# Respacing the attention bursts among the MoE matmuls, pairing a group's first two d_ff chunks in one PSUM tile, and computing the second scores unmixed

## Chip, cores, metric

One core of one Trainium2 chip. The metric is device time in microseconds; lower is better. Compared are fast runs of the same rounds on the same chip. "Stop" below means a pause of TensorE for which the profile names no releaser. A "pair" is a weight load with its matmul. A "page" is a block of 256 instructions, thus some 128 pairs of TensorE's program; a "packet" is the DMA transfer that brings one; a "boundary" is the place in the program where one page ends and the next begins, timed here by the last weight load of the page that ends.

## The reference, cut to what matters

```python
# attention: batch 8, heads 8, seq 576, head_dim 64
# q_d, k_d, v_d: means of 4 neighbouring rows (144 rows)
out = repeat(softmax(q_d k_d^T / 8) v_d, 4) + softmax(mask(|i - j| < 4, q k^T / 8)) v
x   = out as 4608 x 512
h   = x @ w_in                  # 512 x 2048
return (h * sigmoid(1.702 * h)) @ w_out   # 2048 x 512
```

## The kernel before

Nine groups of 512 tokens go through the MoE part, 64 matmuls of 512 columns for each of the two products. The attention of batch g+1 runs inside group g, in bursts of small matmuls put at given places (`POS`, counted in first-product chunks up to 16 and in second-product matmuls from there): scores of four heads and their exponentials (13, 16), scores of the other four heads (35), two bursts of attention times V, "AV" (42, 53), two of transposes (62, 71). Their result xT feeds the next group.

```python
PA = [psum.tile([128, 2, 512], FP32, name=f"pa{i}") for i in range(3)]   # attention, in rotation
PM = [psum.tile([128, 512], FP32, name=f"pm{i}") for i in range(2)]      # MoE, alternating

def scores_mixed(b, qd):
    sp = [ps_tile(), ps_tile()]          # 80 local score matmuls, two tiles
    sd = ps_tile()                       # 24 downsampled ones, a third tile
    ahead = {2 * kc: (lambda kc=kc: scores_d(b, qd, sd, [kc])) for kc in range(3)}
    return scores(b, qd, sp=sp, ahead=ahead), sd      # downsampled first, then in turn
# ... cut ...
def s_pe(qd):
    st["s", qd], st["d", qd] = scores_mixed(b, qd)

def s_act(qd):                           # ScalarE, VectorE
    exp_local(qd, st["s", qd])           # frees the two score tiles
    exp_down(qd, st["d", qd])            # frees the third
    mask_local(qd)
# ... cut ...
def mm1(g, gT, steps, first=0):
    for ffc in range(first, n_ffc):
        for f in steps.get(ffc, ()):
            f()
        hps = pm_tile() if g else acc[ffc] if ffc < 6 else late[ffc - 6]
        for dmc in range(n_dmc):
            hps_mm(g, ffc, dmc, hps)
        silu(gT, ffc, hps)
# ... cut ...
POS = [13, 16, 35, 42, 53, 62, 71]
POS_0 = [16, 18, 30, 48, 52, 57, 66, 70, 75]      # group 0
```

The softmax here doesn't subtract the row's maximum and nothing guards it: scores larger than these inputs give would overflow.

## Time and profile before

| | before |
|---|---|
| median of 3 runs | 323.8 us (323.51 to 324.85) |
| span of the profiled run, clock | 322.0 us, 1.00 |
| TensorE busy | 95% |
| groups 1 to 6, lengths | 34.5, 33.1, 34.3, 34.2, 33.1, 33.7 us |

The group lengths run from a group's first weight load to the next one's. All six hold the same work. The lines of the profile stand in the prediction. Two further sources are the trace's records themselves: the start and length of each 16,384-byte instruction packet, and the start of each weight load, counted from the program's beginning (4860 of them).

### The profile page before, as it was taken

To read this page: it belongs to the slowest core of one execution; us is meant where nothing else is said; L and a number is where in the kernel's file an instruction comes from. 1 tells how busy PE (TensorE), PEld (TensorE's weight loads), DVE (VectorE), ACT (ScalarE), POOL (GpSimd) and SP (SyncE) were. 2 spreads that over 40 slices of the span, in tenths; PEclk is the share of its full clock that TensorE was granted. 3 is DMA by queue.
4 is the path that set the end of the run, shared out by engine and by line. 5 is a ranking of instruction groups with operands and counts; after the bars stand their busy time and mean duration, and the time that the engine had idled before them with its cause. 6 is when DMAs were issued, how large, how long until landed. Compare 5 with 4: busy or idle time off the path is not lost.

```text
span 322.0 us, 10814 instructions
## 1 busy us (share of the span) xinstructions
PE 304.4 (95%) x4806; PEld 156.8 (49%) x4860; DVE 135.5 (42%) x224; ACT 184.0 (57%) x317; POOL 140.0 (43%) x172
## 2 busy tenths in 40 slices
PE   7999989999899999998999989999999999999995
PEld 3664544445444554454545544555445544444444
DVE  6973625912574077505770468027811650000000
ACT  4565762677456674667365836674677456415611
POOL 8993960299009920893059603980296000000000
PEclk9999999999999999999999999999999999999999
DMA  7999999899519941994169714981350210020012
GB/s 117 119 197 209 179 128 212 191 227 238 146 38 200 217 110 66 200 213 116 63 154 212 168 37 129 230 183 55 111 105 0 72 67 0 0 98 34 0 64 69
DMA packets 63550, 40.02 MB, mean 124 GB/s; under 512 B 44048, under 2 KB 54416, under 8 KB 63504
## 3 DMA queue, kind: packets, MB, share of 16 engines
q0 software_dynamic: 18864, 14.95, 32.0%
q1 hardware_dynamic: 44496, 24.32, 31.1%
q8 instruction: 38, 0.62, 0.8%
q14 instruction: 8, 0.07, 0.1%
q10 hardware_dynamic: 144, 0.07, 0.1%
HBM read 44.83 MB, written 9.44 MB: 169 GB/s over the span
## 4 chain that ended last, share of the span: by engine, by line
PE 89%; issue 4%; DMA 4%; DVE 1%; POOL 1%; ACT 0%; POOLq 0%; DVEq 0%
PE pm L702 36%; PE pm L758 34%; PE pa L375 3%; PE pa L702 2%; PE pa L758 2%; DMA qb<-in_q_dram 2%; PE pa L394 2%; PE pa L461 2%; PE pa L502 2%; PE pa L446 2%; DMA vb<-in_v_dram 1%; PE pm L773 1%; PE pa L487 1%; DVE y L478 1%; PE pa L590 1%
## 5 line engine op out<-in xcount | busy, mean ns | idle before, releaser
L702 PE MATMUL pm<-xT,w_in_bf 128*128 128x512 bf16 x527 | 119.7, 379 | 0.7
L758 PE MATMUL pm<-w_out_bf,gT 128*128 128x512 bf16 x493 | 114.3, 379 | 5.3 <-issue 5.1
L713 ACT ACTIVATE gT<-pm 128x512 bf16<-128x512 f32 x136 | 81.1, 598 | 44.0 <-PE pm L702 44.0
L702 PEld LDWEIGHTS <-w_in_bf 128*128 128x128 bf16 x576 | 55.6, 98 | 66.4 <-issue 0.4
L758 PEld LDWEIGHTS <-gT 128*128 128x128 bf16 x560 | 51.6, 98 | 59.6 <-issue 1.4
L425 DVE TENSOR_TENSOR es<-es,mask 128x600 bf16<-128x600 bf16 x28 | 20.2, 733 | 90.6 <-ACT es L411 89.8
L294 POOL TENSOR_TENSOR pq<-kT 128x576 f32<-128x576 bf16 x14 | 16.1, 1148 | 88.5 <-DVE kT L276 88.5
L743 ACT ACTIVATE osb<-pm 128x512 f32<-128x512 f32 (+2 forms) x35 | 20.8, 593 | 36.4 <-PE pm L758 32.4
L617 ACT COPY od<-pa 128x384 f32<-128x384 f32 (+1 forms) x56 | 18.5, 411 | 31.3 <-PE pa L487 25.5
L478 DVE TENSOR_TENSOR y<-pa,rc 128x896 bf16<-128x896 f32 x28 | 30.6, 1092 | 1.0
L638 DVE TENSOR_TENSOR xT<-pa,od 128x570 bf16<-128x570 f32 x28 | 21.1, 753 | 10.3 <-ACT od L617 10.2
L411 ACT ACTIVATE es<-pa 128x600 bf16<-128x600 f32 x32 | 19.7, 667 | 8.8 <-PE pa L375 8.7
L745 DVE TENSOR_SCALAR osb<-pm 128x128 f32<-128x128 f32 x1 | 0.3, 292 | 55.3 <-ACT osb L743 55.3
L314 POOL TENSOR_TENSOR v<-v 112x512 f32<-112x512 f32 x18 | 23.1, 1281 | 0.0
L276 DVE STREAM_TRANSPOSE kT<-kb 128x576 f32<-128x576 f32 x16 | 20.0, 1248 | 3.6 <-DMA kb<-in_k_dram 3.6
L276 DVE STREAM_TRANSPOSE qT<-qb 128x576 f32<-128x576 f32 x16 | 19.9, 1242 | 0.4
L375 PE MATMUL pa<-qT,kT 32*64 32x60 bf16 x1280 | 17.6, 199 | 1.4 <-DVE qT L276 1.4
L375 PEld LDWEIGHTS <-kT 32*64 32x64 bf16 x1280 | 15.9, 103 | 2.0 <-issue 1.5
L230 POOL DMA_DIRECT2D vb<-in_v_dram x20 | 13.7, 697 | 6.5 <-DMA w_in_bf<-in_moe_w_in_dram 4.3
L417 ACT ACTIVATE ed<-pa 128x864 bf16<-128x864 f32 x16 | 14.3, 896 | 2.0 <-PE pa L394 1.8
L394 PE MATMUL pa<-qdT,kdT 32*64 32x144 bf16 x384 | 15.1, 231 | 0.0
L294 POOL TENSOR_TENSOR pq<-qT 128x576 f32<-128x576 bf16 x13 | 15.1, 1159 | 0.0
(98 smaller groups left out, 267.2 us busy)
## 6 DMA issues: line engine op xcount, KB each, us to landing
out_dram<-osb SPq DMA_DIRECT2D x35, 256.0 KB, 2.1
vf<-in_v_dram SPq DMA_DIRECT2D x60, 128.0 KB, 5.2
v<-in_v_dram SPq DMA_DIRECT2D x36, 192.0 KB, 5.1
kb<-in_k_dram POOLq DMA_DIRECT2D x16, 288.0 KB, 7.7
qb<-in_q_dram POOLq DMA_DIRECT2D x16, 288.0 KB, 10.2
w_out_bf<-in_moe_w_out_dram POOLq DMA_DIRECT2D x4, 512.0 KB, 17.6
vb<-in_v_dram POOLq DMA_DIRECT2D x20, 64.0 KB, 5.4
w_in_bf<-in_moe_w_in_dram POOLq DMA_DIRECT2D x2, 512.0 KB, 6.3
```

Of the source, the lines that this page charges most:

```text
L276: nc.vector.transpose(out=t32.rearrange("p (i c) -> p c i", c=18), in_=store[b, qd].bitcast(FP32).rearrange("p (c d) -> p c d", c=18),)
L294: eng.tensor_tensor(out=t1, in0=sv[:, :, 0:2, :], in1=sv[:, :, 2:4, :], op=ALU.add)
L314: eng.tensor_tensor(out=t1[0:112], in0=x[:, :, 0:2, :], in1=x[:, :, 2:4, :], op=ALU.add)
L375: nc.tensor.matmul(sp[r // 2][64 * par : 64 * par + 64, r % 2, 60 * i : 60 * i + 60], lhsT=kT[b, qd][rows, k0 : k0 + 64, a], rhs=qT[b, qd] ...
L394: nc.tensor.matmul(bank[r // 2][64 * j : 64 * j + 64, SD * kc : SD * kc + SD], lhsT=kdT[qd][rows, 48 * kc : 48 * kc + 64, a], rhs=qdT[b, q ...
L425: nc.vector.tensor_tensor(out=ev, in0=ev, in1=mask, op=ALU.mult)
L478: nc.vector.tensor_tensor(out=y[:, xs], in0=ov[:, :, :, 0:D], in1=rc[:, xs].to_broadcast([128, n, 7, D]), op=ALU.mult,)
L638: eng.tensor_tensor(out=sub(xT[hp], t0 + 3, (57, 2), (114, 5), (1, 57)), in0=sub(x, 3, (509, 2), (57, 5), (1, 57)), in1=sub(od, 3, (57, 2) ...
L702: nc.tensor.matmul(acc, lhsT=w_in_bf[:, dmc, ffc * 128 : (ffc + 1) * 128], rhs=xT[dmc][:, g * TG : g * TG + TG], start=(dmc == 0), stop=(d ...
L713: nc.scalar.activation(out=gT[:, ffc, :], in_=acc, func=AF.Silu, scale=GELU_SCALE)
L743: eng.activation(out=osb, in_=ap, func=AF.Copy, scale=1.0 / GELU_SCALE)
L758: nc.tensor.matmul(ops[t], lhsT=gT[:, ffc, t * 128 : (t + 1) * 128], rhs=w_out_bf[:, ffc, :], start=(ffc == 0), stop=(ffc == n_ffc - 1),)
```

## The change

The intent: never so many small matmuls close together, and chunks and scores arranged so that the new places don't wait for ScalarE or xT.

```diff
-            st["s", qd], st["d", qd] = scores_mixed(b, qd)
+            if qd == 0:
+                st["s", qd], st["d", qd] = scores_mixed(b, qd)
+            else:
+                st["s", qd] = scores(b, qd)
+                st["d", qd] = scores_d(b, qd)
@@ mm1
+        if g > 1:
+            t = ps_tile()
+            for dmcs in (range(n_dmc - 1), (n_dmc - 1,)):
+                for ffc in range(2):
+                    for dmc in dmcs:
+                        hps_mm(g, ffc, dmc, t[:, ffc, :])
+            for ffc in range(2):
+                silu(gT, ffc, t[:, ffc, :])
+            first = 2
@@
-    POS = [13, 16, 35, 42, 53, 62, 71]
-    POS_0 = [16, 18, 30, 48, 52, 57, 66, 70, 75]
+    POS = [13, 16, 33, 44, 55, 65, 74]
+    POS_0 = [16, 18, 27, 48, 52, 57, 66, 70, 75]
```

## The prediction

> **What bounds the kernel now.** I read the page first, then the time per group, then the chain of work that ended last, then the single bursts on TensorE. The page:
>
> ```profile
> PE 304.4 (95%) x4806; PEld 156.8 (49%) x4860; DVE 135.5 (42%) x224; ACT 184.0 (57%) x317; POOL 140.0 (43%) x172
> ...
> q8 instruction: 38, 0.62, 0.8%
> ...
> PE 89%; issue 4%; DMA 4%; DVE 1%; POOL 1%; ACT 0%; POOLq 0%; DVEq 0%
> ...
> L702 PE MATMUL pm<-xT,w_in_bf 128*128 128x512 bf16 x527 | 119.7, 379 | 0.7
> L758 PE MATMUL pm<-w_out_bf,gT 128*128 128x512 bf16 x493 | 114.3, 379 | 5.3 <-issue 5.1
> ```
>
> TensorE is the bound: 89% of the chain is its own work. Matmuls overlap, so the 379 ns of one is not its cost: in the chain eight 128x512 matmuls take 1.72 to 1.73 us, so one costs 0.2155 us. 1152 such matmuls (nine groups of 128) make 248 us of 322.0; they, the attention's small matmuls and the head (some 24 us) leave few stalls. Only stalls and the cost of the bursts can change: no matmul is removed. The busy time of each engine in four groups shows how small the pool is:
>
> ```profile
> 95.09:128.21 33.12, 32.22 (x586) 16.56 (x592) 16.46 (x25) 20.95 (x36) 17.54 (x19) 1.00 0.71 144
> 128.21:162.47 34.26, 32.50 (x587) 16.69 (x592) 16.49 (x25) 20.95 (x36) 17.54 (x19) 1.00 0.64 141
> 162.47:196.64 34.17, 32.32 (x586) 16.62 (x592) 16.57 (x25) 20.95 (x36) 17.54 (x19) 1.00 0.65 140
> 196.64:229.73 33.09, 32.19 (x587) 16.55 (x592) 16.42 (x25) 20.95 (x36) 17.54 (x19) 1.00 0.64 145
> ```
>
> The work is the same, the lengths are not: 33.1 against 34.2 us (second column), all at clock 1.00. From the last MoE matmul before a burst to the first after it, less one matmul (each burst also misses one matmul record), a burst costs 1.17 us for the first scores, 1.25 for the second, 0.85 for each pair of attention times V (AV), 0.63 for each pair of transposes: 5.4 us, and 128 x 0.2155 + 5.4 = 33.0, which is the short group. The long ones hold this, in the chain of a window:
>
> ```profile
> 81.33 1.46 PE pm L758 x6
> 82.79 0.22 PE pa L461 x12
> 83.01 0.16 PE pa L446 x20
> 83.16 0.06 PE pa L461 x8
> 83.23 0.95 issue
> 84.18 0.22 PE pa L461 x4
> ```
>
> TensorE stops inside the AV burst, for nothing that another engine releases. Four groups have it (0.95 at 83.2, 0.85 at 150.3, 0.95 at 184.9, 0.27 at 251.9). Counted in weight loads, the stops come after number 1374, 2525, 3164 and 4315: differences of 1151, 640 and 1151, that is 9, 5 and 9 times 128, less 0 to 1. 128 pairs of load and matmul are 256 instructions, and the trace's 38 instruction packets are of 16,384 bytes each. So I read them as **waits for the next page of instructions**. The packet records agree: one ends at 82.79, 149.67, 184.36 and 250.71, and TensorE goes on at 84.18, 151.12, 185.84 and 252.17, 1.39 to 1.48 us later each time. Before these four stops a packet starts 0.9 to 1.7 us after the previous page boundary is executed (at 148.75 4.0 us after it, behind the V loads in small packets) and takes 0.92 to 1.3. A page that is used up in under some 3.5 to 4.2 us therefore stalls. The second scores (104 pairs), 7 MoE matmuls and the first AV (76 pairs) are 187 pairs in about 3.6 us: the one place that dense. In net burst time the stops cost 1.14, 1.05, 1.15 and 0.48 us, with 0.19 and 0.18 in the AV burst after two of them: 4.2 us in all.
>
> One more stall stands in group 0:
>
> ```profile
> 43.59 0.04 ACT es L411
> 43.63 0.53 issue
> 44.16 0.67 ACT es L411
> 44.84 0.04 issue
> 44.88 2.75 PE pa L758 x12
> ```
>
> There token tile 2 accumulates in a PSUM tile that the second scores used; after two MoE matmuls TensorE waits until ScalarE's exponential has read it, from 43.80 (43.58 plus one matmul) to 44.88: 1.08 us.
>
> **The Trainium skill.** "Runtime: NRT & Kernel Launch", Instruction fetch mechanics, says that instructions are refilled in 16 KiB blocks of 256, each engine's sequencer fetching the next through its own DMA queue; packets and spacing here agree. It also says that the fetch is hidden by the sequencer's pace; this trace differs, with 4.2 us of stops. "TensorE: Matmul & The Clock Gate", Wait — 56ns, not 53.3ns?, gives 215.7 ns between warm 512-column matmuls; the chain's 0.2155 agrees. "TensorEngine Tiling (Array Packing)", Key Properties, says that a change of tiling mode drains the array; each burst here loses about 0.09 us before and 0.13 after it. The number of bursts doesn't change, so neither does that. "DMA: Bandwidth & Descriptors", Queues, rings and completion order, has each DMA engine take turns between queues by packet; the late fetch at 148.75, when the V loads thin out, fits only partly.
>
> **The change, part by part.**
> 1. *Spacing.* In groups 1 to 6 the second scores come 2 matmuls earlier, the AVs 2 later, the transposes 3 later. Between second scores and first AV stand 11 MoE matmuls instead of 7: 4 x 0.2155 = 0.86 us more for the fetch. I counted the boundaries through the new instruction order: they stay at the same instruction numbers, so two pairs away within the bursts. The page at 1374 then lasts 3.7 instead of 2.9 us, against 4.2 needed: 0.3 to 0.5 is left of 1.14. That at 3164: 3.7 against 3.9, 0.2 to 0.3 left of 1.15. That at 4316: 3.7 against 3.3, nothing left of 0.48. That at 2525 begins in plain MoE work before the scores, so it gains only 2 matmuls, 0.43 us, and the V loads in front of its fetch may start later: 0.7 left of 1.05. The two small ones stay, 0.37. Left about 1.7 of 4.2: **-2.5 us**. No other page in the new order lasts under 3.7 us.
> 2. *Group 0.* Second scores 3 matmuls earlier (0.65 us), so five stand before tile 2. Unmixed, the 80 local score matmuls end about 0.25 us sooner within the burst, and so the exponential can start. 1.08 - 0.65 - 0.25, less the longer burst, leaves about nothing: **-1.0 us**. Unmixing is also what allows the earlier place: the tile of the downsampled scores is free only at 42.1 us, when its exponential ends (41.20 + 0.90), and the burst would now start at 41.6.
> 3. *Second scores not mixed.* In the head both kinds stand alone: 80 score matmuls take 0.77 us to the next work, 24 downsampled ones 0.51; with 0.09 of entry 1.37 us against 1.17 to 1.25 mixed. Seven times 0.12 to 0.2, less the 0.08 longer entry of the mixed second burst that may go: **+0.5 us**.
> 4. *Two d_ff chunks in a PSUM tile, fourth k step last.* Eight matmuls are reordered, none added. It moves the first use of xT[3] from the 4th to the 7th matmul of a group. Now the last transposes start 2.5 us before the group does, and the merges of xT[2] and xT[3] end 2.2 and 3.1 us after they start. In the new order 6 instead of 9 matmuls follow them: start to group 0.63 + 6 x 0.2155 = 1.9, with xT[2] used at 2.4 (merged 2.2) and xT[3] at 3.2 (3.1). It just fits: **0**. The PSUM tile is the second transpose's of the previous pair, read out more than a microsecond before.
>
> Sum: -2.5 - 1.0 + 0.5 = -3.0; 323.8 - 3.0 = 320.8 us.
>
> **The rivals.** *All fetch stops go:* the spacing may let the sequencer run ahead in the 11 matmuls and ask early; fetches in MoE stretches do start up to 1.3 us before their boundary is executed. Then -4.2 - 1.0 + 0.5: 319.1. *The stops move:* what was gained shows up at other boundaries, or behind the V loads, as the one at 150.3 was; fetch waits differ by over a microsecond from group to group. Then only group 0 and a little remain: 322.3. *A new wait at the start of a group:* the slack of 0.1 to 0.2 us in part 4 fails, because VectorE takes four merges in a row behind ScalarE's copies; 0.2 us in six groups, with later transposes of K and Q delaying GpSimd's pooling (now done 1.3 us before the first scores need it, then 0.7). That would add about 1.5: 322.3.
>
> **Range and chances.** The removable stalls are 4.2 + 1.1 = 5.3 us, or 1.6%, so over 2% faster would need something that the profile doesn't show. The range goes from all stops gone to nearly none. Predicted 320.8 us, 8 in 10 between 318.9 and 322.5; faster by over 2% 0.02, within 2% 0.97, slower 0.01.
>
> **What would show it.** Right: groups 1 to 6 near 33.2 to 33.6 us each; "issue" waits in the first AV gone or under 0.4 us, at weight loads still 128 apart; no wait on ScalarE's exponential in group 0; second scores 0.1 us dearer; no idle time before the first line of a group. Wrong: stops of the same size elsewhere, a wait of the MoE matmuls for xT, or a wait of the scores for GpSimd or ScalarE.

## The result, and the profile after

| | before | after |
|---|---|---|
| median of 5 runs each | 324.1 us | 320.82 us (320.37 to 322.2) |
| ratio of fast runs | | 0.9904 (0.9875 to 0.9932) |
| profiled span | 322.0 us | 319.4 us |
| groups 1 to 6 | 34.5, 33.1, 34.3, 34.2, 33.1, 33.7 | 34.0, 33.2, 33.4, 33.2, 33.2, 33.2 |

The busy time of each engine in groups 1 to 4 of the kernel after (stretch, length, then busy time of TensorE, weight loads, VectorE, ScalarE, GpSimd; clock, DMA share, GB/s):

```profile
60.20:94.23 34.03, 32.58 (x587) 16.67 (x592) 15.54 (x23) 21.41 (x37) 17.73 (x19) 1.00 0.74 176
94.23:127.43 33.20, 32.30 (x586) 16.57 (x592) 16.34 (x25) 20.83 (x36) 17.74 (x19) 1.00 0.69 144
127.43:160.79 33.36, 32.46 (x586) 16.68 (x592) 16.36 (x25) 20.83 (x36) 17.74 (x19) 1.00 0.67 144
160.79:194.00 33.21, 32.31 (x586) 16.57 (x592) 16.43 (x25) 20.83 (x36) 17.75 (x19) 1.00 0.66 144
```

Groups 3 and 4 have come down to the length of the short ones, group 1 only in part. The chain of work in group 1 shows what is left there:

```profile
83.13 0.16 PE pa L446 x20
83.29 0.06 PE pa L461 x6
83.35 0.54 issue
83.89 0.25 PE pa L461 x6
```

It is the same stop after the same weight load, number 1374, now 0.74 us longer than an undisturbed step instead of 1.14. In group 0 a stop of 0.55 us is new in this run, inside the third burst of transposes after weight load 990, 384 = 3 x 128 before 1374. (The kernel before was at the edge there: its packet landed 1.52 us before it was needed, where the stops go on 1.39 to 1.48 us after one. The run b_late below, whose group 0 is that of before, has a stop of 0.3 us at this place.) The wait of group 0 on ScalarE is gone; the same place in the chain (compare the lines of group 0 in the prediction):

```profile
43.06 0.16 issue
43.22 1.03 PE pm L771 x4
44.24 1.94 PE pa L771 x9
```

Token tile 2 (the first `pa L771`) follows without a pause. And something was added: ScalarE at the start of group 2.

```profile
94.43 0.60 ACT L756 ACTIVATE osb<-pm 128x512 f32<-128x512 f32 x1 [0.22 <-PE pm L771]
96.16 1.09 ACT L717 ACTIVATE gT<-pa 128x512 bf16<-128x512 f32 x2 [1.13 <-PE pa L706]
97.12 0.60 ACT L717 ACTIVATE gT<-pm 128x512 bf16<-128x512 f32 x1
```

ScalarE idles for 1.13 us and then gets both paired chunks at once, so it reads the third chunk (97.12) late. The run a_third below shows that this is what costs time: at the 17th matmul of groups 2 to 7 the distance between two MoE matmuls is 0.316 us instead of 0.216; group 8 loses about as much.

Added up from the bursts: stops 4.2 to 1.4 us (0.55 in group 0, 0.74 in group 1, 0.14 in group 3), -2.8; the wait of group 0, -1.08; the second scores, +0.08 in six groups and +0.16 in group 0, +0.64; the pair, seven times 0.1, +0.7. The sum is -2.5 us, where the spans differ by 2.6. The count of stops is rough by 0.2 us: pauses of 0.16 and 0.09 us in the second scores of groups 1 and 2 before are left out, the 0.14 us in those of group 3 after are in.

### The profile page after: what moved, and what is told of

The parts are those of the page before. It is cut to its first block, busy times and chain, and to the rows that moved or that the text cites. A ratio compares the mean times of both kernels' runs of the same rounds, so it can differ in the third digit from the quotient of the medians.

```text
span 319.4 us, 10815 instructions
## 1 busy us (share of the span) xinstructions
PE 305.1 (96%) x4806; PEld 156.9 (49%) x4860; DVE 135.0 (42%) x224; ACT 183.0 (57%) x317; POOL 140.9 (44%) x172
## 4 chain that ended last, share of the span: by engine, by line
PE 90%; DMA 4%; issue 3%; DVE 1%; POOL 1%; ACT 0%; POOLq 0%; DVEq 0%
PE pm L771 35%; PE pm L706 33%; PE pa L706 6%; PE pa L375 3%; PE pa L771 2%; DMA qb<-in_q_dram 2%; PE pa L394 2%; PE pa L461 2%; PE pa L502 2%; DMA vb<-in_v_dram 2%; PE pa L446 1%; PE pm L786 1%; PE pa L487 1%; DVE y L478 1%; PE pa L590 1%
## 5 line engine op out<-in xcount | busy, mean ns | idle before, releaser
L771 PE MATMUL pm<-w_out_bf,gT 128*128 128x512 bf16 x492 | 114.2, 379 | 5.3 <-issue 5.1
L706 PE MATMUL pm<-xT,w_in_bf 128*128 128x512 bf16 x472 | 108.6, 379 | 0.7
L717 ACT ACTIVATE gT<-pm 128x512 bf16<-128x512 f32 x122 | 72.7, 599 | 38.3 <-PE pm L706 38.2
L771 PEld LDWEIGHTS <-gT 128*128 128x128 bf16 x560 | 51.6, 98 | 59.0 <-issue 0.2
L314 POOL TENSOR_TENSOR v<-v 112x512 f32<-112x512 f32 x18 | 24.0, 1331 | 0.0
L706 PE MATMUL pa<-xT,w_in_bf 128*128 128x512 bf16 x88 | 21.1, 379 | 0.1
L717 ACT ACTIVATE gT<-pa 128x512 bf16<-128x512 f32 x22 | 12.2, 604 | 8.5 <-PE pa L706 8.4
L375 PE MATMUL pa<-qT,kT 32*64 32x60 bf16 x1280 | 15.5, 201 | 1.0 <-DVE qT L276 1.0
L375 PEld LDWEIGHTS <-kT 32*64 32x64 bf16 x1280 | 13.8, 103 | 4.6 <-DVE es L425 3.0
```

Source lines behind the costliest of these rows:

```text
L314: eng.tensor_tensor(out=t1[0:112], in0=x[:, :, 0:2, :], in1=x[:, :, 2:4, :], op=ALU.add)
L375: nc.tensor.matmul(sp[r // 2][64 * par : 64 * par + 64, r % 2, 60 * i : 60 * i + 60], lhsT=kT[b, qd][rows, k0 : k0 + 64, a], rhs=qT[b, qd] ...
L706: nc.tensor.matmul(acc, lhsT=w_in_bf[:, dmc, ffc * 128 : (ffc + 1) * 128], rhs=xT[dmc][:, g * TG : g * TG + TG], start=(dmc == 0), stop=(d ...
L717: nc.scalar.activation(out=gT[:, ffc, :], in_=acc, func=AF.Silu, scale=GELU_SCALE)
L771: nc.tensor.matmul(ops[t], lhsT=gT[:, ffc, t * 128 : (t + 1) * 128], rhs=w_out_bf[:, ffc, :], start=(ffc == 0), stop=(ffc == n_ffc - 1),)
```

## The experiments

Two accounts were to be told apart: **F**, that TensorE stops because the next page of instructions isn't there when a page has been used up, and **W**, that the stops belong to the AV burst and what it waits for. When the first results were in, a second question arose: which part of the change ended the stops. All kernels are correct unless it is said. Differences given against the kernel after are those of the two ratios to before, unless the same rounds held both. The profiled runs of a_oldpos, a_nopair and a_mixed have a mean clock of 0.989: the clock record shows half speed for 6.8 us in the head and at the start of group 0. From them only group lengths and waits after that are used. Of the timed runs, two of six of a_oldpos, one of four of a_nopair and two of four of a_mixed have this clock and are 1 to 4 us longer than the others, which stretches the ratios; the differences without them are given too. Where the stops of two kernels are compared, each count is of one profiled run.

**Moving the page boundaries (b_shift48).** The kernel before, with 48 more pairs of weight load and matmul in the head:

```diff
-    warm(4)
+    warm(2)
+    for n in range(52):
+        nc.tensor.matmul(PM[1][:, 0:64], lhsT=zero16[:, 0:128], rhs=zero16[:, 0:64],
+                         start=True, stop=True)
```

> The kernel before with 48 more pairs of weight load and matmul in its head (52 tiny ones in place of two warming matmuls), so that every later page boundary lies 48 pairs earlier in the work. Nothing else changes. Theory F (page fetch): the page that spans second scores and first AV is now short in groups 2 and 5 (boundaries at loads 1966 and 3756 of the old count) and long in groups 1, 3, 4 and 6: groups 2 and 5 grow from 33.1 to about 34.2 us, groups 1, 4 and 6 shrink to about 33.1; group 3 may keep a smaller stop at its transposes. Theory W (a wait for PSUM or another engine in the AV burst): the long groups stay 1, 3, 4 and 6.

Ratio 0.9971 (0.9915 to 1.0027). Groups 1 to 6 last 33.3, 34.5, 33.2, 34.7, 33.9, 33.0 us: groups 1, 3 and 6 have lost their stops, 2 and 5 have got one, after weight loads 2013, 3164 and 3804 (the 48 counted): remainders 93, 92 and 92 modulo 128, the same as before (91 to 94), so the same places in the count and other places in the work. (The remainder sinks because separate waits stand among the pairs in TensorE's queue; with those that the trace records counted as one instruction each, all these stops fall on one place modulo 256, to within one instruction.) The chain in group 2:

```profile
116.51 0.06 PE pa L461 x8
116.57 1.23 issue
117.80 0.22 PE pa L461 x4
```

Put plainly: the stop follows the count of instructions and not the work. That settles F against W. Group 4 was expected to be free and isn't (1.5 us at 183.9): its page lasted long enough, but its packet started only 3.98 us after the boundary before, with about 2,890 of V's 256-byte packets started meanwhile. The length of a page alone doesn't tell where a stop falls.

**The same shift in the changed kernel (a_shift48).**

> The changed kernel with the same 48 pairs in its head. Theory F: the stop of 0.73 us in group 1 and that of 0.54 us in group 0's transposes go, since their boundaries move; the most that groups 2 and 5 can show is 0.5 us each. Group 1 falls from 34.0 to 33.3. In all 0 to 1.3 us faster than the changed kernel, if the head isn't longer. Theory W: the stops stay in groups 0 and 1.

Ratio 0.9898 (0.9837 to 0.9959). Group 1 falls to 33.3 us and no group from 1 to 6 has a stop over 0.3 us; the stop in group 0's transposes goes too. But a new one of 1.0 us comes up inside group 0's second scores (0.86 us of "issue" at 42.69, after weight load 735, 640 = 5 x 128 before 1375). A pause of 0.25 us ahead of those scores is another thing, a wait for the DMA of w_out. The gain in one place is given back in the other. As expected where the stops went; that group 0 would take them up was not seen ahead.

**Old places in groups 1 to 6 (a_oldpos).**

```diff
-    POS = [13, 16, 33, 44, 55, 65, 74]
+    POS = [13, 16, 35, 42, 53, 62, 71]
```

> The changed kernel with the old places of the bursts in groups 1 to 6 (35, 42, 53, 62, 71); group 0, the unmixed second scores and the paired first chunks stay. Theory F (page fetch): the page of the second scores and the first AV lasts 2.8 us again, so the stops come back in groups 1, 3, 4 and 6 at weight loads 128 apart, about 3 us in all less what already remains (0.7): 2.5 to 3.5 us slower than the changed kernel, near 323.5 us. Theory W (what the change gained is group 0 and an earlier exponential through unmixing, the spacing is incidental): within 1 us of the changed kernel.

Ratio 0.9925 (0.9896 to 0.9954), 0.2% or some 0.7 us from the changed kernel (0.4 without the two runs at the lower clock), with intervals that overlap: no difference clear of noise. The 2.5 to 3.5 us of F were wrong, and the time lies within what was written for W. In the profile two of four stops came back, in group 1 (0.6 us) and in group 4:

```profile
187.53 0.09 PE pa L446 x10
187.63 0.85 issue
188.48 0.28 PE pa L446 x9
```

Groups 3 and 6 stay at 33.4 and 33.2 us with the old spacing. So the spacing isn't what ended those. Group 4 is where it shows: with the scores unmixed, both profiled runs with the old places (this one and b_unmix) stop there, for 1.05 and 0.6 us; of the seven with the new places six don't, and best2 has 0.27. Group 1 decides nothing: it stops for 0 to 1.0 us in those seven.

**Only the unmixed second scores (b_unmix).** The kernel before with the first part of the diff alone.

> The kernel before with only the second scores unmixed. Theory: 0.09 us per burst in groups 1 to 6, 0.16 in group 0; the wait of group 0 on the exponential shrinks by 0.25 less the longer burst, the fetch stops shrink a little because the page lasts 0.08 us longer: 0 to 0.5 us slower in all. Rival: the earlier exponential ends the stops in the first AV: 2 us or more faster.

Ratio 0.9903 (0.9854 to 0.9953): as much as the whole change. The expectation was wrong and the rival written beside it right in size. Stops: 1.16 us in group 1, 0.6 in group 4, none in groups 3 and 6. The chain of group 3's first AV, which before held 0.85 us of "issue":

```profile
150.05 0.22 PE pa L461 x12
150.27 0.16 PE pa L446 x20
150.43 0.10 PE pa L461 x12
150.52 0.17 PE pa L446 x19
```

Why, the packets tell. Before, the page needed there began to be fetched 3.98 us after its predecessor's boundary was executed, in group 6 0.92 us after; unmixed, 0.19 and 2.25 us *ahead* of it. In the built program the first weight load of a mixed second burst waits for two engines, GpSimd (pooled K) and ScalarE (the tile of the downsampled scores). The second wait is an instruction of its own in TensorE's queue, and the trace records it: at 147.21 us in group 3, 0.04 us after ScalarE's exponential ends (146.27 + 0.90), and 0.1 us before the burst (a line of `--timeline`, and one of `--source L394` for 147.1 to 147.5 us; `PEldq` is the queue, 51 the length in ns):

```profile
146.27 0.90 ACT L417 ACTIVATE ed<-pa 128x864 bf16<-128x864 f32 x1
L394 PEldq EVENT_SEMAPHORE  x1: 51/51/51, 147.2 to 147.2; - x1
```

Unmixed, it stands after the 80 local score matmuls. Theory **H**: TensorE's sequencer runs ahead of its matmuls, but not past such a wait, and asks for the next page only behind it. The other profiled runs repeat the pattern. In group 6, where no 256-byte packets run, the packet starts 0.7 to 1.2 us after the boundary in the three mixed kernels with this boundary (before, a_mixed, b_late) and 1.3 to 2.3 us ahead of it in all nine unmixed ones; in group 3 3.6 to 4.0 us after, against 0.5 after to 0.7 ahead.

**The second scores mixed again (a_mixed).**

> The changed kernel with the second scores mixed again. Theory: the tile of the downsampled scores is free only when its exponential ends, 0.4 us after the burst starts, so the burst waits 0.4 us in groups 1 to 6 and 0.5 in group 0, the exponential of the local scores is later; the dearer unmixed burst (0.09 in six groups, 0.16 in group 0) goes: 1.5 to 2.5 us slower. Rival: the exponential is done in time, so unmixing only costs: 0.6 us faster.

Ratio 1.0062 (1.0018 to 1.0106): 1.6% or some 5 us slower than the changed kernel (some 4 without the two runs at the lower clock), about twice what was expected. The chain at group 3's second scores:

```profile
150.59 0.79 ACT ed L417
151.39 0.14 issue
151.52 0.24 PE pa L394 x2
```

The burst waits for the downsampled exponential: the gap of weight loads before it is 1.00 us in each of six groups instead of 0.52. That was expected. Not expected: stops return in groups 3, 4 and 6 beside the one in group 1 (0.44, 0.23, 0.77 and 0.46 us for groups 1, 3, 4 and 6). As mixing with the new places leaves 1.9 us of stops, and unmixing with the old ones 1.8, each of the two takes away more than half of it alone. The stops in the AV bursts of groups 1 to 6, one profiled run each:

| | mixed | unmixed |
|---|---|---|
| old places | 4.2 us (before) | 1.8 (b_unmix), 1.7 (a_oldpos) |
| new places | 1.9 (a_mixed) | 0.7 (after; 0.9 with the 0.14 in second scores) |

**The wait met earlier, still mixed (b_late).**

```diff
-    POS = [13, 16, 35, 42, 53, 62, 71]
+    POS = [13, 16, 38, 45, 56, 63, 71]
```

> The kernel before with the second scores and all after them 2 or 3 matmuls later (38, 45, 56, 63, 71): still mixed, still 7 matmuls between second scores and first AV. Theory H (the mixed second burst has a separate wait of TensorE's sequencer on ScalarE at its head, which in the kernel before is met only 0.1 us ahead of the burst, so the sequencer cannot run ahead into it and asks for the next page late; unmixing moved that wait 80 pairs into the burst): here the wait is met about 0.6 us earlier than the burst, so the sequencer passes it ahead of time: in groups 3 and 6 the packet starts before its boundary is executed instead of 4.0 and 0.9 us after, and their stops of 1.05 and 0.48 us go; groups 1 and 4, whose boundary lies 20 to 38 pairs inside the burst, keep 0.5 to 1.2 us each. 1 to 2.5 us faster than before. Theory S (only the distance of 7 matmuls counts): the four stops stay. Theory M (mixing itself slows the fetch): they stay too.

Ratio 0.9942 (0.9897 to 0.9986), a gain of the size expected, but not by the way expected. In group 3 the packet still starts 3.58 us after the boundary, in group 6 0.72 after; group 6 keeps 0.4 us, groups 1 and 4 keep 0.9 each, and group 3's stop in the first AV fell from 1.05 to 0.2 us, which fits that its page holds three more MoE matmuls. What was expected of the packets was wrong, for a reason that fits H: the separate wait is recorded at 146.86, right when ScalarE ends (145.93 + 0.90), and the packet starts at 148.01, 1.15 us behind it; in group 6 247.11 and 248.51. In the kernel before these distances are 1.54 (group 3) and 1.06 us (group 6). A request issued 0.7 us before the burst can't bring a packet before it if a packet takes over 1.1 us to start. What H says, that the fetch follows the wait, holds in both kernels. Theory S alone doesn't explain the sizes, since the distance is 7 here too; Theory M isn't excluded, since three of four stops stay.

In group 3 two things remain. The boundary is executed 10 pairs (13 here) *before* the burst, so ahead of the wait, and H as worded doesn't say why a request for which the boundary is passed should still be held up. And V's 256-byte packets, some 2,400 since the boundary, run out just when the packet starts (148.5 us before, 148.0 here); they can't be the whole cause, as the unmixed kernels load the same V, but they may be part of the delay.

A second witness is in the trace of before: the *first* scores are mixed as well but have no separate wait at their head, and a boundary 12 pairs into that burst in group 6 has its packet 0.06 us after it, where one 5 pairs into the second burst has it 0.92 after; neither has other DMA traffic around it. A run that removes only the wait and leaves the order mixed was not made, so H is supported by timing, best in group 6, and not isolated.

**Without the V loads of batches 3 to 7 (a_nov, wrong result on purpose, one run of unknown state).**

```diff
-                load_v(b + 1)
+                vf[b + 1] = vf[b]
```

> The changed kernel without the loads of V for batches 3 to 7 (wrong result on purpose: the V of batch 2 is used again). Theory: what is left of the stop in group 1 (0.73 us; 0 to 1.2 in the other runs) comes from its packet standing behind V's 256-byte packets: it goes, and the packets that follow the first scores start within 2.5 us of their boundary instead of 3.3 to 4.5. The stop in group 0 (0.54 us) stays, V of batch 2 is still loaded. Rival: the fetch is late whatever else is loaded: both stay.

Group 1 lasts 33.3 us; its first AV runs through:

```profile
82.99 0.22 PE pa L461 x12
83.21 0.16 PE pa L446 x20
83.36 0.10 PE pa L461 x12
83.46 0.17 PE pa L446 x19
```

Its packet starts 1.03 us after the boundary instead of 2.03. That fits the expectation, but this one run doesn't show it: with V's loads in place the packet starts 1.06 us after in a_nopair, which has no stop there, 1.17 in best2 and up to 2.64 in a_third. In group 0 0.3 us are left at the transposes; a pause of 0.9 us behind its first AV, at 49.3, is no page stop but a wait for the DMA of w_out. The delay after the first scores is 3.67 us in group 1, where the V loads had not begun, and 2.55 in group 2, both over the 2.5 us expected; in groups 4 and 5 it is 1.5 and 1.2 us, where the kernel after has 3.3 and 4.5. So V's loads go with most of the delay in the later groups but not in group 1; K's and Q's loads or the sequencer remain possible causes there.

**Without the paired chunks (a_nopair).** `if g > 1` became a condition that is never true.

> The changed kernel without the two first chunks in a PSUM tile. Theory: the merge of the fourth xT ends 3.1 us after the last transposes start, and it would now be used 0.63 + 6 x 0.2155 + 3 x 0.2155 = 2.6 us after: a wait of 0.4 to 0.6 us at the 4th matmul of six groups, while the 0.1 us wait at the 17th matmul of seven groups goes: 2 to 3 us slower. Rival: the merges are early enough anyway and the pair only costs: 0.7 us faster.

Ratio 1.0009 (0.996 to 1.0057), about 3.4 us slower than the changed kernel, or 2.7 without its run at the lower clock, in the middle of what was expected. TensorE at the start of group 2:

```profile
98.46 1.24 PE L706 MATMUL pm<-xT,w_in_bf 128*128 128x512 bf16 x5 [0.48 <-DVE xT L644]
```

The fourth matmul waits for the merge of the fourth xT, 0.64 us more than an undisturbed step, in each of groups 2 to 7. The groups after the first last 33.75 us instead of 33.2. So with the last transposes at 74 the pair is needed.

**The third chunk in another tile (a_third).**

```diff
-            hps = pm_tile() ...
+            hps = ps_tile()[:, 0, :] if g > 1 and ffc == 2 else pm_tile()
```

> The changed kernel with a group's third d_ff chunk in one more PSUM tile of the rotating three. Theory: the 0.1 us wait at the 17th matmul of seven groups is for ScalarE, which gets both paired chunks at once and so reads the third chunk late, whose PSUM tile the fifth chunk needs; with another tile it goes: 0.7 us faster, the gap of 0.316 us in each group becomes 0.216. Rival: the wait is for the fourth xT or for the output copy of the last token tile: nothing changes.

The distance of 0.316 us is gone from all groups, and groups without a stop last 33.11 instead of 33.21 us: the wait was for ScalarE's reading. The ratio, 0.9881 (0.981 to 0.9952), doesn't show 0.7 us clearly: this profiled run has stops of 1.0 us each in groups 0 and 1, and one of the four runs has clock 0.989.

**Group 0's second scores back at 30 (a_oldpos0).**

> The changed kernel with only the second scores of group 0 back at 30. Theory: the wait of token tile 2 on the exponential returns, 0.65 us of it (unmixing keeps 0.25 and costs 0.16), and the new stop of 0.54 us inside group 0's third transposes stays or moves by a few pairs: 0.3 to 0.8 us slower. Rival: the new stop was caused by the earlier place (the fetch of its page was asked for at another time), so it goes and the two cancel: no difference.

Ratio 0.991 (0.9878 to 0.9941), 0.2 us from the changed kernel: inconclusive as a time. In the trace the wait on the exponential is back with 0.56 us (1.08 mixed at the same place), and the stop in the transposes stays with 0.8, which speaks against the rival's reason; group 1 happened to have none.

**A version from these findings (best2), beside the changed kernel again (after_5).** No pair, unmixed scores, the new distance to the first AV, the last transposes where they were:

```diff
-    POS = [13, 16, 33, 44, 55, 65, 74]
+    POS = [13, 16, 33, 44, 55, 63, 71]
```

> The changed kernel without the paired first chunks and with its last bursts as early as before (33, 44, 55, 63, 71), so that no chunk has to wait for xT and ScalarE doesn't get two chunks at once. Theory: the 0.1 us per group of the pair goes, seven times, and no wait at the start of a group comes; stops as in the changed kernel: 0.5 to 1 us faster than it in the same rounds, some 319.5 to 320.5 us, unless the transposes, now 8 apart, make a page short.

> The changed kernel again, for a comparison on the same chip in the same rounds: ratio to before 0.988 to 0.993. Its spans show how far the stops in groups 0 and 1 vary from run to run: 0 to 1.2 us each.

best2: 320.09 us median, ratio to before 0.987 (0.9832 to 0.9908). after_5: 320.77 us, 0.9901 (0.9863 to 0.9939). best2 is the fastest median; the means of the same rounds differ by 0.3% (six runs each, with ranges that overlap), so its lead isn't clear of noise. Its groups without stops last 33.1 us; in its profiled run groups 1 to 6 have only two small stops (0.24 us in group 1, 0.27 in group 4), but group 0 has one of 1.0. after_5's profiled run has 0.4 us in group 0 and 0.5 in group 1.

## Why the prediction was right, by its steps

That the number was met to 0.02 us (320.8 against 320.82) is luck. The kernel after alone ranges over 1.8 us; the base was 323.8 us for the prediction and 324.1 with five runs; and added up from the profiled bursts the change is worth -2.5 us, not -3.0: the pair cost 0.7 us that the sum doesn't have, and stops gave 0.3 more than it has. The reading of the bound was right, the account of the parts only in part.

- *Stops are page fetches.* Right, and shown by b_shift48: the stops moved with the instruction count.
- *Spacing, -2.5 us.* The size holds for spacing alone: 1.7 us were to be left, and a_mixed has 1.9. But the step took it for the only part of the change that acts on stops. b_unmix has 1.8 left without any spacing. Together they leave 0.9 in groups 1 to 6; beside the unmixed scores the spacing is worth some 0.9 us of stops, and no time that is clear of noise (a_oldpos). Its measure, that a page used up in under 3.5 to 4.2 us stalls, failed both ways: group 0's page lasted 4.5 us and the stop came, as the packet started 2.5 us after its boundary; and in group 2 before, a page of 3.1 us ended without a stop, its packet 0.5 us ahead of the boundary. Nor do fetches in MoE stretches start at most 1.3 us ahead of their boundary, as the rival says: the one at 283.11 us was 3.9 us ahead. It was also wrong on where: 0.7 us was to be left in group 3 (0.14), 0.3 to 0.5 in group 1 (0.74), 0.2 to 0.3 in group 4 (none).
- *Second scores not mixed, +0.5 us.* The step that failed. Its cost was measured at +0.64 us, close to what was said, but only the cost was counted: the separate wait at the head of the mixed burst, visible before as an entry 0.08 us longer, was read as a trifle. By the timing of the packets it held up the request for the next page, which no run isolates. What is shown is that the part alone gains 1% (b_unmix) and so is worth more than its cost.
- *Group 0, -1.0 us.* Right: the wait of 1.08 us is gone and the unmixed order was what allowed it. But 0.55 us came back 14 us later at a page boundary in the transposes, at a place where the kernel before was at the edge; the step didn't look there.
- *Pair, 0.* xT arrives in time, as worked out, and a_nopair shows the wait that the pair avoids. The cost of 0.7 us came from an engine that the step didn't follow: ScalarE receives two chunks at once. It was named among the rivals as a new wait at a group's start, with the wrong engine behind it.
- *Rivals.* "All stops gone" and "the stops move" each came true in places: gone or nearly so in groups 3, 4 and 6, new in group 0.

Open: whether the separate wait alone, without the order of the mixed burst, holds up the fetch, and how, where the boundary lies ahead of it; and why the packet after the first scores still starts 1.2 to 3.7 us late without V loads.

## What to carry to other kernels

Where TensorE pauses with no releaser, count its instructions between pauses: multiples of one page point to instruction fetch, and a few dummy pairs in the head test it: if the pauses move with the count, it is the fetch. Then try both remedies that worked here: put more large matmuls between dense bursts of small ones, and don't begin a burst with an operation that has to wait for two engines at once. Test each part of a change alone, as the part that counted here was booked as a cost. When several chunks are finished together, follow the engine that reads them, not only the data they wait for.

## What the Trainium skill lacked or had wrong

- "Runtime: NRT & Kernel Launch", Instruction fetch mechanics, has the fetch hidden by the sequencer's pace. Here it cost 4.2 us of 322.0 before and 1.4 of 319.4 after. The section gives no latency: a packet took 0.88 to 1.85 us in the fourteen profiled runs, once 2.68, and TensorE went on 1.39 to 1.48 us after the packet's end in the four stops before.
- No page read says whether a separate semaphore wait in TensorE's queue holds up the page request. The timing here suggests it and doesn't isolate it: packets started 0.92 and 3.98 us after their boundary with it at the burst's head, 2.25 and 0.19 us ahead with it 80 pairs later.
- "DMA: Bandwidth & Descriptors", Queues, rings and completion order, describes turns between queues by packet. What that means for instruction packets it doesn't say: the one after group 5's first scores started 4.5 us after its boundary beside V's 256-byte packets and 1.2 without, in one run each.
- "TensorEngine Tiling (Array Packing)", Key Properties, names the drain at a change of mode but no cost: before, TensorE lost about 0.09 us into a burst (0.14 into the mixed second scores) and 0.13 out of it. That this is the drain alone, no run shows.
